# VectorE's score banks moved into three-bank iterations, with 30 sets of exponentials

## The chip, the cores and the metric

The kernel runs on one NeuronCore of one Trainium2 chip. The metric is the device time of one launch in microseconds (us). A profiled execution is one such launch with the hardware profiler on; its span runs from the first to the last instruction.

## The reference

Two branches act on the same kind of input, and a gate mixes them. Branch A is softmax attention with 32 heads of 20 columns over 2048 positions, branch B is a dense layer, a mish, and a dense layer.

```python
x = A_x                                  # 1 x 2048 x 640, bfloat16
g = sigmoid((x * gate_w).sum(-1, keepdims=True))

# branch A: H = 32 heads, Dh = 20
q, k, v = split_heads(x @ wqkv)          # each 1 x 32 x 2048 x 20
p = softmax(einsum("bhqd,bhkd->bhqk", q, k) * Dh ** -0.5)
a = merge_heads(einsum("bhqk,bhkd->bhqd", p, v)) @ wo

# branch B: F = 1536
h = B_x @ w1 + b1
b = (h * tanh(softplus(h))) @ w2         # softplus as log1p(exp(-|h|)) + max(h, 0)

return g * a + (1 - g) * b
```

The kernel reads one x for both branches.

## The kernel before

**Tiling.** Four heads make one value of `p` (eight in all), and a head's 20 columns sit on 32 partitions, so that four heads fill 128. The 2048 queries are cut into four chunks `qc` of 512, the keys into 16 blocks `j` of 128. A pair `(p, qc)` is a *group* `G`; there are 32 groups, in the order of the list `groups`. In a group, a *unit* is one block of keys of one head: 128 keys by 512 queries, one PSUM bank of scores. A *set* is the four units (four heads `t`) of one `j`. There are 32 x 16 x 4 = 2048 units.

**The inner loop.** Units are dealt to iterations of three and two banks in turn (`WIDTHS = (3, 2)`). `emit_qk` issues an iteration's score matmuls (L1070) into the PSUM tile S0 (three banks) or S1 (two banks); `emit_exp` issues one ScalarE instruction over the whole tile (L1081) and writes the exponentials to `E`; `emit_set` multiplies a set of four units into `acc` (L1128). A score matmul uses 32 rows of the array, the rows of its head, and the matmuls of one iteration go to different heads. The value tile `VA` has a column of ones per head, so `acc` also holds the softmax's denominator; `normalise` transposes it (L1096), inverts (L1102), multiplies (L1105, into `T2`) and transposes back (L1114).

**VectorE's exponentials.** In the 27 groups of `JV_GROUPS` the last set (`j = 15`) does not go to ScalarE. `jv_chain` issues one score matmul (L702) into a bank of the general pool `pp`, and a VectorE instruction (L711) that rounds the scores to 16-bit integers in `E_dve`. After the fourth, `jv_steps` lists seven VectorE instructions on all four units at once (128x2048, L730 to L752) that turn the integers into bfloat16 exponentials with the temporaries `w_dve` and `u_dve`. `emit_jv` then multiplies them with `VB`, which is `VA`'s block scaled by a power of two on GpSimd (`scale_v`, L1230).

**What sets the order.** The schedule is written out by the Python program itself: every engine runs its instructions in the order of issue. The program keeps an estimated time for each engine in `T` and decides by it. All other work is cut into `Chain`s: the projections for q and k (L464, read at L475 and L479) and v (L492, L505), the dense layers of branch B (L581 and L612, read at L592 and L624), the output projection (L657, L674), the bound checks (L798), and the four `jv_chain`s of a group. A chain has a start, a due iteration and a lead by which it is sorted (24 for `jv_chain`), takes one of the two banks of `pp`, and ends in a VectorE read of that bank (`evac`). After each iteration `pump` issues pieces of chains, as far as the estimated end of the next exponential allows; where nothing else can run and the estimated activity of TensorE is below 0.54 it issues filler matmuls on the tile `busy` (L1014). VectorE's longer sequences (mish at L530 to L562, the normalising, `jv_steps`) wait in the list `slow`; `run_slow` issues those steps that fit ahead of a given time, the earliest deadline first.

```python
S_full[i] = T["pe"] + NS_SCORES_SEEN
...
limit = T["act"] + NS_EXP[iters[min(i + 1, NI - 1)][1]] - NS_SCORES_SEEN - 60.0
```

A second path, `attention_with_maximum`, follows for inputs that fail a bound; it does not run here.

Of the kernel before, what the change touches and what calls it, by code (L numbers as in the profile page):

```python
# [9 lines left out]
P = 128  # L10
ACT = mybir.ActivationFunctionType
ALU = mybir.AluOpType
# [138 lines left out]
def kernel(  # L151
# [25 lines left out]
    LN2 = 0.6931471805599453  # L177
    Q_SCALE = 512.0 * float(DH) ** -0.5 / LN2
    WIDTHS = (3, 2)
    JV_GROUPS = list(range(4, 31))  # L180
    JV_BIAS = 32
    LEAD_JV = 24
    N_CAP = 1.0e9
    NCELL = 48
    CELLS_KEPT = 2
# [32 lines left out]
    ident = consts.tile([P, P], BF16, tag="ident")  # L218
    wqp = [consts.tile([P, KT, 4, 32], BF16, tag=f"wqp{i}", name=f"wqp{i}") for i in range(2)]
    wkp = [consts.tile([P, KT, 4, 32], BF16, tag=f"wkp{i}", name=f"wkp{i}") for i in range(2)]  # L220
    T2 = [consts.tile([P, QC], BF16, tag=f"T2_{i}", name=f"T2_{i}") for i in range(2)]
    cells = [consts.tile([P, QC], BF16, tag=f"cell{i}", name=f"cell{i}") for i in range(NCELL)]
    busy = consts.tile([P, P], BF16, tag="busy")
    xn = consts.tile([P, NQC], F32, tag="xn")
    wn = consts.tile([P, NQ, 2], F32, tag="wn")
    vn = consts.tile([P, 3], F32, tag="vn")
    F16, I16 = mybir.dt.float16, mybir.dt.int16
    E_dve = consts.tile([P, 4, QC], BF16, tag="E_dve")
    w_dve = consts.tile([P, 4, QC], F16, tag="w_dve")
    VB = consts.tile([P, H, DH + 1], BF16, tag="VB")  # L230
    u_dve = consts.tile([P, 4, QC], F16, tag="u_dve")
    b_dram = tc.dram_tile([S, D], BF16, name="b_dram")
    acc = accpool.tile([P, QC], F32, tag="acc")

# [26 lines left out]
        if u < 2:  # L261
            load_strip(1 - u, 0, eng)
    make_identity(nc, ident)
    warm = consts.tile([P, 1], F32, tag="warm")
    nc.vector.memset(warm, 0.0)
    nc.vector.memset(busy, 1.0)
    nc.scalar.activation(warm, warm, ACT.Exp)
    for t in (wqp[0], wkp[0], VA[:, :, :, DH : DH + 1], wqp[1], wkp[1], T2[0], T2[1]):
        nc.vector.memset(t, 1.0 if len(t.shape) == 4 and t.shape[-1] == 1 else 0.0)
    nc.gpsimd.dma_start(out=wv0[:, :, :], in_=wrows[:, :, 2 * D : 2 * D + 4 * DH])  # L270
    for c in range(1, NQC):
# [27 lines left out]
    for G, (p, qc) in enumerate(groups):  # L299
        first.setdefault(p, G)  # L300

    JV = NS - 1
    with_jv = [G in JV_GROUPS for G in range(len(groups))]
    units = [
        (G, p, qc, j, t)
        for G, (p, qc) in enumerate(groups)
        for j in range(NS)
        if not (with_jv[G] and j == JV)
        for t in range(4)
    ]  # L310
    unit_at = {(G, j): k for k, (G, _, _, j, t) in enumerate(units) if t == 0}
    iters = []
    pos = 0
    while pos < len(units):
        n = min(WIDTHS[len(iters) % len(WIDTHS)], len(units) - pos)
        iters.append((pos, n))
        pos += n
    NI = len(iters)
    it_of = [0] * len(units)
    for i, (a, n) in enumerate(iters):  # L320
# [72 lines left out]
            full = pp.tile([P, QC], F32, tag="pp", name="ps")  # L393
        return full

    def steps(start, parts, deadline):


        seq[0] += 1
        slow.append([deadline, seq[0], start, deque(parts)])  # L400

    def run_slow(limit):

        while True:
            todo = [x for x in slow if max(T["dve"], x[2]) + x[3][0][0] <= limit]
# [284 lines left out]
    EXP_A, EXP_B = 17.79869142, 3.99584201  # L690
    EXP_C = 0.0057399568925583745
    ROUND = 1.5 * 2.0**23
    jv_free = [True]
    jv_at = {}

    def jv_chain(G, p, t, start, due):
        box = {}
        bank = opener(box, QC)

        def piece():  # L700
            jv_free[0] = False
            nc.tensor.matmul(  # L702
                bank()[:, :],
                lhsT=kT[p][32 * t : 32 * t + 32, JV * P : (JV + 1) * P],
                rhs=qT[G][32 * t : 32 * t + 32, :],
                tile_position=(32 * t, 0),
            )

        def finish():
            evac(690)  # L710
            nc.vector.tensor_scalar(  # L711
                out=E_dve.bitcast(I16)[:, t, :], in0=box["ps"][:, :], scalar1=ROUND,
                scalar2=ROUND - 512.0 * JV_BIAS, op0=ALU.add, op1=ALU.subtract,
            )
            if t == 3:
                left = (it_at(G + 1) - now[0]) * 1115.0
                steps(T["dve"], jv_steps(G), T["act"] + left - 4000.0)

        def ready():
            return G in qT and (jv_free[0] if t == 0 else not jv_free[0])  # L720

        return Chain(start, due, [(215, piece)], finish, ready, hard=False, bank=bank, lead=LEAD_JV)

    def jv_steps(G):
        V = nc.vector
        E, w, u = (t.rearrange("p a n -> p (a n)") for t in (E_dve, w_dve, u_dve))
        e, wi = E.bitcast(I16), w.bitcast(I16)

        def mantissa():
            V.tensor_scalar(  # L730
                out=wi, in0=e, scalar1=511, scalar2=0x4000, op0=ALU.bitwise_and, op1=ALU.bitwise_or
            )

        def exponent():
            V.tensor_scalar(
                out=e, in0=e, scalar1=-512, scalar2=2, op0=ALU.bitwise_and, op1=ALU.logical_shift_right
            )

        def square():
            V.tensor_tensor(out=w, in0=w, in1=w, op=ALU.mult)  # L740

        def factor():
            V.tensor_scalar(out=u, in0=w, scalar1=EXP_A, scalar2=EXP_C, op0=ALU.add, op1=ALU.mult)

        def factor2():
            V.tensor_scalar(out=w, in0=w, scalar1=EXP_B, scalar2=None, op0=ALU.add)

        def product():
            V.tensor_tensor(out=w.bitcast(BF16), in0=w, in1=u, op=ALU.mult)

        def scale():
            V.tensor_tensor(out=e, in0=e, in1=wi, op=ALU.add)  # L752
            jv_at[G] = T["dve"] + NS_SEEN

        return [
            (700, mantissa), (700, exponent), (1230, square), (700, factor), (700, factor2),
            (1230, product), (1230, scale),
        ]


# [131 lines left out]
    for G, (p, qc) in enumerate(groups):  # L892
        if with_jv[G]:
            for t in range(4):
                x = it_at(G) + 1 + 2 * t
                chains.append(jv_chain(G, p, t, x, x + 2))

    def spread(a, b, n):
        return [(a + (b - a) * k / n, a + (b - a) * (k + 1) / n) for k in range(n)]
# [152 lines left out]
    E_of = {}  # L1052
    S_free = {}
    S_full = {}
    E_full = {}
    late = [0.0]

    def emit_qk(i):
        a, n = iters[i]
        w = WIDTHS[i % len(WIDTHS)]  # L1060
        tag = f"S{i % len(WIDTHS)}"
        ps = spool.tile([P, w * QC], F32, tag=tag, name="Sp")
        S_of[i] = ps
        T["pe"] = max(T["pe"], S_free.get(tag, 0.0))
        S_full[i] = T["pe"] + NS_SCORES_SEEN
        worked(T["pe"], 215.0, 0.5)
        T["pe"] += NS_SCORES
        for k in range(n):
            G, p, qc, j, t = units[a + k]
            nc.tensor.matmul(  # L1070
                ps[:, k * QC : (k + 1) * QC],
                lhsT=kT[p][32 * t : 32 * t + 32, j * P : (j + 1) * P],
                rhs=qT[G][32 * t : 32 * t + 32, :],
                tile_position=(32 * t, 0),
            )

    def emit_exp(i):
        a, n = iters[i]
        which = i % len(WIDTHS)
        E = ep[which].tile([P, WIDTHS[which] * QC], BF16, tag=f"E{which}", name="E")  # L1080
        nc.scalar.activation(  # L1081
            E[:, 0 : n * QC], S_of.pop(i)[:, 0 : n * QC], ACT.Exp, scale=LN2 / 512.0
        )
        late[0] += max(0.0, S_full[i] - T["act"])
        T["act"] = max(T["act"], S_full.pop(i)) + NS_EXP[n]
        S_free[f"S{i % len(WIDTHS)}"] = T["act"] + NS_EXP_SEEN
        for k in range(n):
            E_of[a + k] = E[:, k * QC : (k + 1) * QC]
            E_full[a + k] = T["act"] + NS_EXP_SEEN

    def normalise(G, p, qc):
# [6 lines left out]
        t2 = T2[G % 2]  # L1098
        OT[(p, qc)] = cells.pop()

        def invert():
# [16 lines left out]
    pv_next = [0]  # L1118
    pv_group = [(0, 0, 0)]
    pv_sets = [0]  # L1120
    jv_in = [False]

    def emit_set(G, p, qc, j, moving, full, VB=None):
        n = pv_sets[0]
# [12 lines left out]
        if n == NS - 1:  # L1137
            normalise(G, p, qc)
            pv_sets[0] = 0
            jv_in[0] = False  # L1140

    def emit_jv(G, p, qc):
        jv_in[0] = jv_free[0] = True
        emit_set(G, p, qc, JV, lambda t: E_dve[:, t, :], jv_at[G], VB)

    def emit_pv(limit):
        count = 0
        while True:
# [8 lines left out]
            if with_jv[G] and not jv_in[0]:  # L1157
                last = pv_sets[0] == NS - 1
                if last and full and G not in jv_at:
                    run_slow(float("inf"))  # L1160
                if pv_sets[0] > 0 and (jv_at.get(G, 1e9) <= T["pe"] + 60.0 or (last and full)):
                    emit_jv(G, p, qc)
                    count += 1
                    continue
# [62 lines left out]
        )  # L1227

    def scale_v(h0, h1):
        nc.gpsimd.tensor_scalar(  # L1230
            out=VB[:, h0:h1, :], in0=VA[:, JV, h0:h1, :], scalar1=2.0**-JV_BIAS, scalar2=None,
            op0=ALU.mult,
        )

    def clear_wo(p):
        if p == 0:
# [7 lines left out]
            nc.sync.dma_start(out=wo_sb[0][32 * t : 32 * t + DH, :, :], in_=rows[t])  # L1244

    at(it_at(first[1]) + 2, gate_values)
    at(it_at(first[1]), lambda: scale_v(4, 16))
    at(it_at(first[4]), lambda: scale_v(16, H))
    at(it_at(1), lambda: nc.vector.tensor_copy(b1f, b1bf))
# [91 lines left out]
```

## Time and profile before

| what | value |
|---|---|
| three timed runs | 945.32 us median, 940.99 to 949.07 |
| the profiled execution | 954.2 us, span 952.3 us |
| granted TensorE clock, mean over the span | 0.962 |
| ScalarE busy | 912.2 us (96%) |
| TensorE matmuls busy | 863.2 us (91%) |
| VectorE busy | 694.3 us (73%) |
| GpSimd busy | 21.7 us (2%) |
| first and last exponential (L1081) | start at 10.4 us, end at 941.2 us |

Busy time is the union of an engine's instructions. In the rows of the profile, the part after the first bar is busy time and mean duration of one instruction, the part after the second is the time the engine stood idle just before these instructions, with the instruction that ended most of it. Matmuls overlap in the array, and a ScalarE instruction's record can begin before its neighbour's has ended, so a mean duration is not the distance from one to the next. A table by stretches gives start and end of a stretch, its length, the busy time and the count of instructions of each engine in it, then the granted TensorE clock and two DMA columns.

### The profile page before, as it was taken

How to read it: one execution, taken by the hardware profiler on the slowest of the kernel's cores; microseconds unless marked ns; L12 is line 12 of the kernel's file. 1: busy time of each engine (PE TensorE's matmuls, PEld its weight loads, DVE VectorE, ACT ScalarE, POOL GpSimd, SP SyncE). 2: the span in 40 equal slices, each digit the busy share in tenths (PEclk: the TensorE clock that was granted, in tenths of full speed). 3: DMA queues.
4: the chain of work that ended last, by engine and by line, in shares of the span. 5: the costliest groups of instructions: out<-in, count | busy, mean ns of one | idle time of the engine just before them, and what ended most of it. 6: DMA issues, size and time to landing. Idle time of an engine off the chain costs nothing.

```text
span 952.3 us, 14757 instructions
## 1 busy us (share of the span) xinstructions
PE 863.2 (91%) x6073; PEld 298.8 (31%) x6073; DVE 694.3 (73%) x1156; ACT 912.2 (96%) x830; POOL 21.7 (2%) x35
## 2 busy tenths in 40 slices
PE   8999989999998888899899989898999899999996
PEld 4443322222233232322223222232223223333332
DVE  4335487777888888777788988788787877876533
ACT  6999998989999999989999999999999989999995
POOL 5000010000000000000000000000000000000000
PEclk9999997979999999979999999999999989999998
DMA  9000010000100010001011001010000000000100
GB/s 289 8 1 1 21 30 1 18 4 1 31 4 19 2 30 1 21 1 50 1 30 35 22 1 30 1 50 1 21 1 21 1 1 15 35 15 9 42 28 30
DMA packets 25632, 21.96 MB, mean 23 GB/s; under 512 B 10089, under 2 KB 24313, under 8 KB 25561
## 3 DMA queue, kind: packets, MB, share of 16 engines
q1 hardware_dynamic: 22808, 14.28, 5.5%
q0 software_dynamic: 1520, 5.94, 2.0%
q8 instruction: 48, 0.79, 0.3%
q10 hardware_dynamic: 1232, 0.76, 0.3%
q14 instruction: 24, 0.19, 0.1%
HBM read 15.73 MB, written 5.24 MB: 22 GB/s over the span
## 4 chain that ended last, share of the span: by engine, by line
ACT 61%; issue 18%; PE 18%; DVE 1%; DMA 1%; POOL 1%; ACTq 0%; POOLq 0%
ACT E L1081 58%; PE Sp L1070 5%; PE acc L1128 3%; ACT e L522 3%; PE ps L657 2%; PE ps L612 2%; PE ps L581 2%; PE ps L464 2%; DMA wv<-in_A_wqkv_dram 1%; PE ps L702 1%; PE ps L1014 0%; PE ps L492 0%; DVE ot L1291 0%; DVE h L592 0%; POOL xs L272 0%
## 5 line engine op out<-in xcount | busy, mean ns | idle before, releaser
L1081 ACT ACTIVATE E<-Sp 128x1536 bf16<-128x1536 f32 (+1 forms) x776 | 894.5, 1351 | 21.9 <-PE Sp L1070 20.8
L1070 PE MATMUL Sp<-qT,kT 32*128 32x512 bf16 x1940 | 313.2, 392 | 76.6 <-ACT E L1081 65.5
L1070 PEld LDWEIGHTS <-kT 32*128 32x128 bf16 x1940 | 104.0, 91 | 306.4 <-issue 287.9
L1128 PE MATMUL acc<-E,VA 128*21 128x512 bf16 x1940 | 196.6, 395 | 0.8 <-DVE T L1096 0.8
L1128 PEld LDWEIGHTS <-VA 128*21 128x21 bf16 x1940 | 47.8, 89 | 113.0 <-issue 112.7
L711 DVE TENSOR_SCALAR E_dve<-ps 128x512 int16<-128x512 f32 x108 | 71.8, 678 | 12.7 <-PE ps L702 12.3
L581 PE MATMUL ps<-xT,w1t 128*128 128x512 bf16 x240 | 80.3, 406 | 0.0
L1014 PE MATMUL ps<-busy 128*128 128x512 bf16 x246 | 75.5, 389 | 0.0
L612 PE MATMUL ps<-w_sb,cell 128*128 128x320 bf16 x384 | 75.3, 307 | 0.0
L592 DVE TENSOR_SCALAR h<-ps,b1f 128x512 f32<-128x512 f32 x48 | 35.8, 746 | 37.5 <-PE ps L581 37.2
L464 PE MATMUL ps<-xT,wkp 128*128 128x512 bf16 x155 | 49.1, 405 | 1.7 <-DVE xT L430 0.8
L464 PE MATMUL ps<-xT,wqp 128*128 128x512 bf16 x155 | 48.4, 392 | 0.0
L657 PE MATMUL ps<-wo_sb,cell 128*128 128x320 bf16 x248 | 46.9, 305 | 0.0
L544 DVE RECIPROCAL r<-r 128x128 f32<-128x128 f32 x48 | 45.4, 945 | 1.0
L479 DVE CAST kT<-ps 128x512 bf16<-128x512 f32 x31 | 21.4, 690 | 32.2 <-PE ps L464 32.1
L475 DVE TENSOR_SCALAR qT<-ps 128x512 bf16<-128x512 f32 x31 | 21.4, 692 | 27.1 <-PE ps L464 26.9
L612 PEld LDWEIGHTS <-cell 128*128 128x128 bf16 x384 | 30.0, 98 | 34.3 <-issue 27.6
L1096 DVE STREAM_TRANSPOSE T<-acc 128x512 f32<-128x512 f32 x32 | 22.9, 715 | 23.0 <-PE acc L1128 22.8
L702 PE MATMUL ps<-qT,kT 32*128 32x512 bf16 x108 | 38.3, 387 | 0.0
L522 ACT ACTIVATE e<-h 128x512 f32<-128x512 f32 x48 | 35.5, 739 | 0.7 <-DVE h L592 0.7
L505 DVE CAST VA<-ps 128x80 bf16<-128x80 f32 (+2 forms) x48 | 16.4, 378 | 25.0 <-PE ps L492 24.9
L553 DVE TENSOR_TENSOR e<-e,r 128x512 f32<-128x512 f32 x48 | 33.2, 692 | 1.6
(107 smaller groups left out, 694.3 us busy)
## 6 DMA issues: line engine op xcount, KB each, us to landing
w1t<-in_B_w_dram SPq DMA_DIRECT2D x14, 480.0 KB, 3.7
b_dram<-Bt SPq DMA_DIRECT2D x4, 640.0 KB, 3.1
out_dram<-ot SPq DMA_DIRECT2D x14, 160.0 KB, 1.8
xs<-in_A_x_dram POOLq DMA_DIRECT2D x3, 640.0 KB, 6.7
w_sb<-in_B_w_dram POOLq DMA_DIRECT2D x1, 1920.0 KB, 12.6
ws<-in_A_wqkv_dram SPq DMA_DIRECT2D x13, 100.0 KB, 3.9
w1t<-in_B_w_dram POOLq DMA_DIRECT2D x2, 480.0 KB, 8.8
wo_sb<-in_A_wo_dram SPq DMA_DIRECT2D x4, 200.0 KB
```

The costliest lines, as they stand in the source:

```text
L464: nc.tensor.matmul(box["ps"][:, :], lhsT=wpad[:, kt, :, :].rearrange("p h d -> p (h d)"), rhs=xT[:, kt, chunk * QC : (chunk + 1) * QC], st ...
L522: nc.scalar.activation(e[:, :], h[:, :], ACT.Exp)
L544: V.reciprocal(out=r[:, Q], in_=r[:, Q])
L581: nc.tensor.matmul(box["ps"][:, :], lhsT=w1t[4 * c + ft // 3][:, kt, (ft % 3) * P : (ft % 3 + 1) * P], rhs=xT[:, kt, c * QC : (c + 1) * QC ...
L612: nc.tensor.matmul(box["ps"][:, :], lhsT=act[(ft, c)][:, u * P : (u + 1) * P], rhs=w2_sb[:, ft, half * HALF : (half + 1) * HALF], start=(f ...
L657: nc.tensor.matmul(box["ps"][:, :], lhsT=OT[(p, c)][:, u * P : (u + 1) * P], rhs=wo_sb[0][:, p, cols], start=(k == 0), stop=(k == len(ps_l ...
L702: nc.tensor.matmul(bank()[:, :], lhsT=kT[p][32 * t : 32 * t + 32, JV * P : (JV + 1) * P], rhs=qT[G][32 * t : 32 * t + 32, :], tile_positio ...
L711: nc.vector.tensor_scalar(out=E_dve.bitcast(I16)[:, t, :], in0=box["ps"][:, :], scalar1=ROUND, scalar2=ROUND - 512.0 * JV_BIAS, op0=ALU.ad ...
L1014: nc.tensor.matmul(ps[:, 0:n], lhsT=busy[:, :], rhs=busy_row(n), start=True, stop=True)
L1070: nc.tensor.matmul(ps[:, k * QC : (k + 1) * QC], lhsT=kT[p][32 * t : 32 * t + 32, j * P : (j + 1) * P], rhs=qT[G][32 * t : 32 * t + 32, :] ...
L1081: nc.scalar.activation(E[:, 0 : n * QC], S_of.pop(i)[:, 0 : n * QC], ACT.Exp, scale=LN2 / 512.0)
L1128: nc.tensor.matmul(acc[32 * t : 32 * t + DH + 1, :], lhsT=VA[:, j, 4 * p + t, :] if VB is None else VB[:, 4 * p + t, :], rhs=moving(t), st ...
```

## The change

- The score matmul of VectorE's set no longer goes through a chain and a bank of `pp`. In 120 of the three-bank iterations ScalarE takes two banks, and the third bank is a score of VectorE's set. `JV_GAPS` says how many iterations pass before each of a group's four; `t` is chosen among the heads left, at first from those that the iteration does not already use.
- `jv_read` issues VectorE's read of that bank right behind the score matmuls of the iteration. The PSUM tile is free for the next scores when ScalarE and VectorE have both read it.
- VectorE's set is in 30 groups (1 to 30), one set each, where there were 27 (4 to 30).
- `E_dve` has two buffers; `w_dve` and `u_dve` hold two units instead of four; the seven steps run once for each half of a set (128x1024), the first half after the second read. The halves are kept in order by the name `"exp"` in `run_slow`.
- `VB` holds two blocks, and `scale_v` fills both; it is called once more, for the first four heads. `T2` is one tile instead of two, and `warm` is a column of `xn`.

```diff
-    JV_GROUPS = list(range(4, 31))
+    JV_SETS = {G: 1 for G in range(1, 31)}
     JV_BIAS = 32
-    LEAD_JV = 24
+    JV_GAPS = {1: (4, 2, 4, 2), 2: (3, 2, 2, 2, 2, 2, 2, 2)}
...
-    E_dve = consts.tile([P, 4, QC], BF16, tag="E_dve")
-    w_dve = consts.tile([P, 4, QC], F16, tag="w_dve")
-    VB = consts.tile([P, H, DH + 1], BF16, tag="VB")
-    u_dve = consts.tile([P, 4, QC], F16, tag="u_dve")
+    E_dve = [consts.tile([P, 4, QC], BF16, tag=f"E_dve{i}", name=f"E_dve{i}") for i in range(2)]
+    w_dve = consts.tile([P, 2, QC], F16, tag="w_dve")
+    VB = consts.tile([P, 2, H, DH + 1], BF16, tag="VB")
+    u_dve = consts.tile([P, 2, QC], F16, tag="u_dve")
...
     while pos < len(units):
-        n = min(WIDTHS[len(iters) % len(WIDTHS)], len(units) - pos)
+        i = len(iters)
+        G = units[pos][0]
+        n = min(WIDTHS[i % len(WIDTHS)], len(units) - pos)
+        x = None
+        got = taken_by.setdefault(G, [])
+        sets_here = len(mine_of[G])
+        if n == 3 and len(got) < 4 * sets_here:
+            since = i - (got[-1][0] if got else iters_start.get(G, i))
+            if since >= JV_GAPS[sets_here][len(got)] and units[pos + 1][0] == G:
+                mine = {units[pos][4], units[pos + 1][4]}
+                k, slot = divmod(len(got), 4)
+                left = [t for t in range(4) if t not in [y for _, y in got[4 * k :]]]
+                t = min(left, key=lambda t: (t in mine, t))
+                got.append((i, t))
+                x = (G, units[pos][1], k, t, slot)
+                n = 2
...
+        extra.append(x)
         pos += n
...
-    def jv_chain(G, p, t, start, due):
...
+    def jv_read(G, k, t, slot, ps, full):
+        if slot == 0:
+            n = jv_set[(G, k)] = len(jv_set)
+            assert n < 2 or n - 2 in jv_emitted, (G, k)
+        n = jv_set[(G, k)]
+        jv_slot[(G, k, t)] = slot
+        run_slow(full + 100.0)
+        vec(690, full)
+        nc.vector.tensor_scalar(
+            out=E_dve[n % 2].bitcast(I16)[:, slot, :], in0=ps, scalar1=ROUND,
+            scalar2=ROUND - 512.0 * JV_BIAS, op0=ALU.add, op1=ALU.subtract,
+        )
+        if slot % 2 == 1:
+            left = (it_at(G + 1) - now[0]) * 1115.0
+            due = T["act"] + (min(left - 4000.0, 9000.0) if k < len(mine_of[G]) - 1 else left - 4000.0)
+            steps(T["dve"], jv_steps(G, k, slot // 2), due, "exp")
...
-            (700, mantissa), (700, exponent), (1230, square), (700, factor), (700, factor2),
-            (1230, product), (1230, scale),
+            (380, mantissa), (380, exponent), (640, square), (380, factor), (380, factor2),
+            (640, product), (640, scale),
...
     def emit_qk(i):
...
+        todo = [(units[a + k][0], units[a + k][1], units[a + k][3], units[a + k][4]) for k in range(n)]
+        if extra[i] is not None:
+            G, p, k, t, slot = extra[i]
+            todo.append((G, p, mine_of[G][k], t))
+        for k, (G, p, j, t) in enumerate(todo):
...
+        if extra[i] is not None:
+            G, p, k, t, slot = extra[i]
+            jv_read(G, k, t, slot, ps[:, n * QC : (n + 1) * QC], S_full[i])
+            S_read[i] = T["dve"] + 60.0
...
+        if i in S_read:
+            S_free[tag] = max(S_free[tag], S_read.pop(i))
...
     def scale_v(h0, h1):
-        nc.gpsimd.tensor_scalar(
-            out=VB[:, h0:h1, :], in0=VA[:, JV, h0:h1, :], scalar1=2.0**-JV_BIAS, scalar2=None,
-            op0=ALU.mult,
-        )
+        for k in range(2):
+            nc.gpsimd.tensor_scalar(
+                out=VB[:, k, h0:h1, :], in0=VA[:, NS - 1 - k, h0:h1, :], scalar1=2.0**-JV_BIAS,
+                scalar2=None, op0=ALU.mult,
+            )
...
+    at(it_at(1), lambda: scale_v(0, 4))
```

More of the change, by code (lines that the diff above doesn't have):

```diff
@@ L220 @@
     wkp = [consts.tile([P, KT, 4, 32], BF16, tag=f"wkp{i}", name=f"wkp{i}") for i in range(2)]
-    T2 = [consts.tile([P, QC], BF16, tag=f"T2_{i}", name=f"T2_{i}") for i in range(2)]
+    T2 = consts.tile([P, QC], BF16, tag="T2")
     cells = [consts.tile([P, QC], BF16, tag=f"cell{i}", name=f"cell{i}") for i in range(NCELL)]
@@ L263 @@
     make_identity(nc, ident)
-    warm = consts.tile([P, 1], F32, tag="warm")
+    warm = xn[:, 0:1]
     nc.vector.memset(warm, 0.0)
@@ L267 @@
     nc.scalar.activation(warm, warm, ACT.Exp)
-    for t in (wqp[0], wkp[0], VA[:, :, :, DH : DH + 1], wqp[1], wkp[1], T2[0], T2[1]):
+    for t in (wqp[0], wkp[0], VA[:, :, :, DH : DH + 1], wqp[1], wkp[1], T2):
         nc.vector.memset(t, 1.0 if len(t.shape) == 4 and t.shape[-1] == 1 else 0.0)
@@ L300 @@
         first.setdefault(p, G)
-    JV = NS - 1
-    with_jv = [G in JV_GROUPS for G in range(len(groups))]
+    mine_of = [[NS - 1 - k for k in range(JV_SETS.get(G, 0))] for G in range(len(groups))]
     units = [
@@ L307 @@
         for j in range(NS)
-        if not (with_jv[G] and j == JV)
+        if j not in mine_of[G]
         for t in range(4)
@@ L312 @@
     iters = []
+    extra = []
     pos = 0
+    taken_by, iters_start = {}, {}
     while pos < len(units):
-        n = min(WIDTHS[len(iters) % len(WIDTHS)], len(units) - pos)
+        i = len(iters)
[14 more added lines that the diff above has]
+                n = 2
+        for k in range(pos, pos + n):
+            iters_start.setdefault(units[k][0], i)
         iters.append((pos, n))
+        extra.append(x)
         pos += n
+    assert all(len(taken_by[G]) == 4 * len(mine_of[G]) for G in range(len(groups)))
     NI = len(iters)
@@ L394, in take_bank, with steps @@
         return full
-    def steps(start, parts, deadline):
+    def steps(start, parts, deadline, line=None):
         seq[0] += 1
-        slow.append([deadline, seq[0], start, deque(parts)])
+        slow.append([deadline, seq[0], start, deque(parts), line])
     def run_slow(limit):
         while True:
-            todo = [x for x in slow if max(T["dve"], x[2]) + x[3][0][0] <= limit]
+            heads = {}
+            for x in slow:
+                heads.setdefault(x[4] or x[1], x)
+            todo = [x for x in heads.values() if max(T["dve"], x[2]) + x[3][0][0] <= limit]
             if not todo:
@@ L692, with jv_steps @@
     ROUND = 1.5 * 2.0**23
-    jv_free = [True]
+    jv_set = {}
     jv_at = {}
-    def jv_chain(G, p, t, start, due):
[L697 to L706, printed above, removed]
-            )
[L709 to L724, printed above, removed]
+    jv_slot = {}
+    halves = {}
+    jv_emitted = set()
+    def jv_read(G, k, t, slot, ps, full):
[14 more added lines that the diff above has]
+            steps(T["dve"], jv_steps(G, k, slot // 2), due, "exp")
+    def jv_steps(G, k, half):
         V = nc.vector
-        E, w, u = (t.rearrange("p a n -> p (a n)") for t in (E_dve, w_dve, u_dve))
+        E, w, u = (
+            t.rearrange("p a n -> p (a n)")
+            for t in (E_dve[jv_set[(G, k)] % 2][:, 2 * half : 2 * half + 2, :], w_dve, u_dve)
+        )
         e, wi = E.bitcast(I16), w.bitcast(I16)
@@ L752, in scale @@
             V.tensor_tensor(out=e, in0=e, in1=wi, op=ALU.add)
-            jv_at[G] = T["dve"] + NS_SEEN
+            halves[(G, k)] = halves.get((G, k), 0) + 1
+            if halves[(G, k)] == 2:
+                jv_at[(G, k)] = T["dve"] + NS_SEEN
         return [
-            (700, mantissa), (700, exponent), (1230, square), (700, factor), (700, factor2),
-            (1230, product), (1230, scale),
+            (380, mantissa), (380, exponent), (640, square), (380, factor), (380, factor2),
+            (640, product), (640, scale),
         ]
@@ L890 @@
         )
[L892 to L896, printed above, removed]
     def spread(a, b, n):
@@ L1054 @@
     S_full = {}
+    S_read = {}
     E_full = {}
@@ L1067, in emit_qk @@
         T["pe"] += NS_SCORES
-        for k in range(n):
-            G, p, qc, j, t = units[a + k]
+        todo = [(units[a + k][0], units[a + k][1], units[a + k][3], units[a + k][4]) for k in range(n)]
[3 more added lines that the diff above has]
+        for k, (G, p, j, t) in enumerate(todo):
             nc.tensor.matmul(
@@ L1085, in emit_exp @@
         T["act"] = max(T["act"], S_full.pop(i)) + NS_EXP[n]
-        S_free[f"S{i % len(WIDTHS)}"] = T["act"] + NS_EXP_SEEN
+        tag = f"S{i % len(WIDTHS)}"
+        S_free[tag] = T["act"] + NS_EXP_SEEN
+        if i in S_read:
+            S_free[tag] = max(S_free[tag], S_read.pop(i))
         for k in range(n):
@@ L1097, in normalise @@
         rec = tp.tile([P, NS], F32, tag="rec", name="rec")
-        t2 = T2[G % 2]
+        t2 = T2
         OT[(p, qc)] = cells.pop()
@@ L1120 @@
     pv_sets = [0]
-    jv_in = [False]
+    jv_in = [0]
     def emit_set(G, p, qc, j, moving, full, VB=None):
@@ L1139, in emit_set @@
             pv_sets[0] = 0
-            jv_in[0] = False
+            jv_in[0] = 0
     def emit_jv(G, p, qc):
-        jv_in[0] = jv_free[0] = True
-        emit_set(G, p, qc, JV, lambda t: E_dve[:, t, :], jv_at[G], VB)
+        k = jv_in[0]
+        n = jv_set[(G, k)]
+        jv_in[0] += 1
+        jv_emitted.add(n)
+        E = E_dve[n % 2]
+        emit_set(
+            G, p, qc, mine_of[G][k], lambda t: E[:, jv_slot[(G, k, t)], :], jv_at[(G, k)], VB[:, k, :, :]
+        )
     def emit_pv(limit):
@@ L1156, in emit_pv @@
             G, p, qc = pv_group[0]
-            if with_jv[G] and not jv_in[0]:
-                last = pv_sets[0] == NS - 1
-                if last and full and G not in jv_at:
+            k = jv_in[0]
+            if k < len(mine_of[G]):
+                last = pv_sets[0] == NS - len(mine_of[G]) + k
+                if last and full and (G, k) not in jv_at:
                     run_slow(float("inf"))
-                if pv_sets[0] > 0 and (jv_at.get(G, 1e9) <= T["pe"] + 60.0 or (last and full)):
+                if pv_sets[0] > 0 and (jv_at.get((G, k), 1e9) <= T["pe"] + 60.0 or (last and full)):
                     emit_jv(G, p, qc)
@@ L1229, in scale_v @@
     def scale_v(h0, h1):
-        nc.gpsimd.tensor_scalar(
-            out=VB[:, h0:h1, :], in0=VA[:, JV, h0:h1, :], scalar1=2.0**-JV_BIAS, scalar2=None,
-            op0=ALU.mult,
-        )
+        for k in range(2):
+            nc.gpsimd.tensor_scalar(
+                out=VB[:, k, h0:h1, :], in0=VA[:, NS - 1 - k, h0:h1, :], scalar1=2.0**-JV_BIAS,
+                scalar2=None, op0=ALU.mult,
+            )
     def clear_wo(p):
```

## The prediction

> **What bounds the kernel now.** I read the page first (busy shares and the chain that ended last), then ScalarE's rows with shapes kept apart, then the stretches where the granted clock was one half, and last TensorE's rows in the window just ahead of such a stretch. The page:
>
> ```profile
> span 952.3 us, 14757 instructions
> PE 863.2 (91%) x6073; PEld 298.8 (31%) x6073; DVE 694.3 (73%) x1156; ACT 912.2 (96%) x830; POOL 21.7 (2%) x35
> PEclk9999997979999999979999999999999989999998
> ACT E L1081 58%; PE Sp L1070 5%; PE acc L1128 3%; ACT e L522 3%; PE ps L657 2%; PE ps L612 2%; PE ps L581 2%; PE ps L464 2%; DMA wv<-in_A_wqkv_dram 1%; PE ps L702 1%; PE ps L1014 0%; PE ps L492 0%; DVE ot L1291 0%; DVE h L592 0%; POOL xs L272 0%
> L711 DVE TENSOR_SCALAR E_dve<-ps 128x512 int16<-128x512 f32 x108 | 71.8, 678 | 12.7 <-PE ps L702 12.3
> L702 PE MATMUL ps<-qT,kT 32*128 32x512 bf16 x108 | 38.3, 387 | 0.0
> ```
>
> The line of exponentials on ScalarE (L1081) is the chain. Its two shapes:
>
> ```profile
> L1081 ACT ACTIVATE E<-Sp 128x1536 bf16<-128x1536 f32 x388 | 607.8, 1567 | 6.4 <-PE Sp L1070 5.8
> L1081 ACT ACTIVATE E<-Sp 128x1024 bf16<-128x1024 f32 x388 | 440.6, 1136 | 15.5 <-PE Sp L1070 15.0
> ```
>
> The rows' means overlap their neighbours, so I took end to end from the trace: the medians are 1343 ns for three banks, 916 for two and 510 for the exponential at L522. So one bank is 427 ns and an instruction 62. The work is 388 x (1.343 + 0.916) + 48 x 0.51 = 901.0 us. From the first start at 10.4 us to the last end at 941.2 us there are 930.7 us, so **29.7 us** of ScalarE's time are lost. Of them 22.1 us lie in and just behind nine stretches, 64.9 us long together, in which TensorE had half its clock; 2.6 us lie before 40 us; the rest is scattered. Three of the nine stretches, and TensorE's rows in the 3.41 us ahead of one:
>
> ```profile
> core 0: us, PE busy (x) PEld busy (x) DVE busy (x) ACT busy (x) POOL busy (x), PEclk, DMA share, GB/s
> 138.47:155.54 17.07, 16.03 (x73) 3.82 (x72) 11.34 (x19) 12.95 (x11) 0.00 (x0) 0.50 0.08 16
> ...
> 404.71:418.37 13.66, 13.66 (x60) 3.18 (x59) 8.39 (x14) 10.17 (x10) 0.00 (x0) 0.50 0.01 1
> ...
> 466.15:469.57 3.42, 3.42 (x16) 0.73 (x14) 1.59 (x4) 2.31 (x2) 0.00 (x0) 0.50 0.00 0
> ```
> ```profile
> L1070 PE MATMUL Sp<-qT,kT 32*128 32x512 bf16 x8 | 1.2, 380 | 0.9 <-ACT E L1081 0.7
> L581 PE MATMUL ps<-xT,w1t 128*128 128x512 bf16 x2 | 0.8, 486 | 0.0
> L1128 PE MATMUL acc<-E,VA 128*21 128x512 bf16 x8 | 0.8, 386 | 0.0
> L702 PE MATMUL ps<-qT,kT 32*128 32x512 bf16 x2 | 0.8, 379 | 0.0
> L464 PE MATMUL ps<-xT,wqp 128*128 128x512 bf16 x1 | 0.4, 379 | 0.0
> ```
>
> In a stretch ScalarE is busy 71 to 76% and TensorE nearly always. Ahead of it TensorE is not idle either, but the work is thin: the two L702 matmuls stand alone on 32 rows, and almost nothing uses the whole array (L464 once; L581 reaches in at the end). I cut the span from 30 to 935 us at full clock into the same 3.41 us windows, on whose grid all stretches begin and end. 173 windows hold no L702 matmul, and none of them was followed by half clock. 25 hold at least about two, and nine of these were, all nine cases. The share of a window that matmuls on the full array stream is 5 to 12% ahead of the nine, 33% in the median of the 173. So the thin phase is made by the four score matmuls of VectorE's set: each takes a bank of the two general ones, waits for VectorE to free it, and keeps other work out meanwhile.
>
> **The change, part by part.**
>
> *ScalarE's work.* Three more groups go to VectorE: 12 banks less, 1928 instead of 1940. But 120 three-bank iterations now give ScalarE only two. Following the list-building code by hand, there are 819 iterations: 290 of three banks, 529 of two. 290 x 1.343 + 529 x 0.916 = 874.0 against 876.5: **-2.5 us** (12 x 0.427 saved, 43 more instructions at 0.062 paid).
>
> *The lone score matmuls.* The 108 at L702 and their claims on the two general banks go; the scores ride in an iteration whose three matmuls take 0.39 us together, as one alone does. In 30 of the 120 the third shares its 32 rows with one of the other two and may run after it, at most 30 x 0.39 = 11.7 us of TensorE; it lies behind the 0.47 us by which three-bank scores are ready before ScalarE (median in the trace). The freed pieces go to full-array work. A pair with an extra bank is 1.83 us long; two score sets and one set at L1128 take 1.2 us by the 0.39 rows, but only 0.33 each start to start as the timeline has them, so 0.6 to 0.8 us remain, two to three pieces of 0.22 us (four at L464 in the trace start within 0.65 us). That is a quarter to a third of full-array work where the nine windows had 5 to 12%. So I let the half-clock stretches go: bounds 0 and **-22.1 us**; I take the whole, and leave room for about one stretch of the new kernel's own, 22.1 / 9 = 2.5 us, taken as **+2 us**.
>
> [...] The windows above show the clock halved after TensorE had been busy 2.4 to 2.9 of 3.41 us, so here I go by the trace.
>
> *The score bank waits for VectorE.* This is the new wait. The bank triple is free when ScalarE and the read (0.68, L711) are both done; behind a late read stand the next three scores and with them all of TensorE, and on VectorE itself the copies out of the general banks. Budget: scores are full 0.05 + 0.39 us after the previous exponential on the triple ends; the two-bank exponential in between ends 0.47 later, the triple's own 0.92 later. 1.39 - 0.68 = 0.71 us of lateness hold nothing, and 0.47 more only eat the slack: ScalarE idles from 1.19 us on. How late are such reads now? From the end of the L702 matmul to the start of L711 it is 0.19 us in the median, 0.63 at 90%, 1.06 at most at full clock. So the lower price is nothing; the upper, a tenth of 120 reads late by 0.3 us beyond the budget, is 3.6. I take **+2 us**.
>
> *VectorE's steps.* These rows price the halves:
>
> ```profile
> L740 DVE TENSOR_TENSOR w_dve<-w_dve 128x2048 f16<-128x2048 f16 x27 | 32.8, 1216 | 0.0
> ...
> L531 DVE TENSOR_SCALAR r<-e 128x512 f32<-128x512 f32 x48 | 20.7, 431 | 1.7
> ...
> L735 DVE TENSOR_SCALAR E_dve<-E_dve 128x2048 int16<-128x2048 int16 x27 | 18.6, 689 | 0.5
> ```
>
> A set now takes 4 x 0.69 + 3 x 1.22 = 6.41 us. Instructions on 128x1024 of two bytes are not in the trace; exact halves would be 3.2 us a half set, no saving 6.41. The nearest rows have the same bytes: L531 0.431, and L553 with two sources 0.692. So a half is 4 x 0.431 + 3 x 0.692 = 3.80, a set 7.60. 30 x 7.60 - 27 x 6.41 = +55 us (bounds +19 and +212), and 12 more reads +8: VectorE goes from 694 to 757 us, 81% of the span. It is off the path: groups 4 to 30 use some 21 to 25 us of 28 to 30, and get 1.2 more; the three early groups use 12.5 to 19 and get 10.3. The cover is its idle time, 258 us, most of it waits for TensorE. The two-fold E_dve takes away the wait for the previous set; the single T2 and w_dve, u_dve are used on VectorE alone, in its order: 0.
>
> *GpSimd.* scale_v issues six instructions instead of two, about 1 us each (L1230, 0.95), at a 2% busy engine, over 5 us ahead of their reader: 0. No DMA is added or moved. One memset less ahead of the first exponential, 0.27 us that lie beside the input's DMAs: 0.
>
> **Sum.** The profiled execution took 954.2 us with a span of 952.3. 954.2 - 2.5 - 22.1 + 2 + 2 = 933.6. The three runs have a median of 945.32 and a lowest of 940.99: the profiled execution is 9 above, and its own lost time is what varies. With less half clock in the plain runs there is less to win, but the end is the same floor, 929.6 with no stretch and 933.6 with my two additions. I go between, toward the floor since plain runs lie below the profiled one: **931 us**, own range 922 to 936.
>
> **The rivals.** (a) *Half clock stays.* The stretches follow a group's start by 5 to 10 us, where other things happen too (the normalising, L1096), and 16 of the 25 windows did not trip; if these set it, only -2.5 + 2 remains: 945 us. For it: two-bank pairs give fewer pieces per iteration. Against: no window without L702 tripped. Chance 0.18. (b) *VectorE becomes the bound*, slower. Place: groups 4 to 30, reads at fixed iterations behind mish steps. Now those groups have 22 to 25 us of work and the waits for TensorE beside it (some 208 us by the groups' idle rows, 6.5 each): 29 of 28 to 30. If the waits do not shrink when 1.2 us come in, each of 27 groups grows by about 1.1, 30 us on 931: 961 us. It decides where reads start later than 1.19 us after the scores. Against: most reads start within 0.33. Chance 0.12. (c) The change not doing what it says would be scores still alone; the list has 120 extras, so I leave it no share.
>
> **How the numbers follow.** Forecast 0.70, (a) 0.18, (b) 0.12. The range reaches down to the floor with all 29.7 us back, 954.2 - 29.7 - 2.5 = 922, one less for scatter, and up past (a) to 948: 921 to 948, leaving out (b) and little else. About 1% is what a measurement of this kernel can tell from no change: 935.9 to 954.8. Faster gets 0.66 of the forecast and 0.02 of (a); same 0.04, 0.16 and 0.02 of (b); slower 0.10.
>
> **What would show it.** Right: clock near 1.0 through the middle; two ACTIVATE rows, 290 and 529; idle before L1081 under 8 us; VectorE near 757; reads of the third bank starting within 0.7 us. Wrong: half-clock stretches some 5 to 10 us into groups (a), or scores waiting on the read, with TensorE idle "<-DVE E_dve" over 20 us (b).

## The result and the profile after

The changed kernel takes **981.56 us** (median of 4 runs, 980.70 to 982.79); the kernel before, beside it, 944.60. The ratio is 1.039, 95% interval 1.034 to 1.044: slower by 4%, where I had forecast 931 us. The ratios, here and below, leave out executions more than 1.5% above the fastest of the same kernel; the medians are over all.

The page of the changed kernel, with the lines that answer to those shown of before (L1107 is the exponential, L734 VectorE's read, L1092 the scores):

```profile
span 979.4 us, 15290 instructions
PE 874.1 (89%) x6184; PEld 311.6 (32%) x6184; DVE 744.3 (76%) x1398; ACT 916.8 (94%) x873; POOL 24.4 (2%) x39
PEclk9999999999999999999999999999999999999998
ACT E L1107 52%; PE Sp L1092 8%; DVE E_dve L734 7%; ACT e L548 3%; PE acc L1157 2%; PE ps L490 2%; PE ps L638 1%; PE ps L607 1%; DMA wv<-in_A_wqkv_dram 1%; DVE h L618 1%; PE ps L518 0%; PE ps L683 0%; DVE ot L1329 0%; DVE T L1125 0%; DVE kT L505 0%
```

Two things stand out. The clock row is full until the last slice (mean 0.995), as forecast. And VectorE's read L734 has 7% of the chain, where L711, VectorE's read of before, is not among the lines shown. ScalarE's rows and the head of the chip's waits (engine, line, whom it waited for, us in total, times, longest) tell where it sits:

```profile
L1107 ACT ACTIVATE E<-Sp 128x1024 bf16<-128x1024 f32 x529 | 548.5, 1061 | 43.3 <-DVE E_dve L734 40.8 <-PE Sp L1092 1.3 <-PE acc L1157 1.0
L1107 ACT ACTIVATE E<-Sp 128x1536 bf16<-128x1536 f32 x290 | 438.2, 1511 | 0.8 <-PE Sp L1092 0.8
```
```profile
DVE E_dve L734 <- PE Sp L1092: 62.2, 93, 1.5
ACT E L1107 <- DVE E_dve L734: 40.8, 107, 1.5
```

ScalarE's exponential waits for VectorE's read *of the other bank of the same tile*, 107 times. VectorE itself is not late: it sits idle ahead of 93 of its 120 reads until the scores are there. One extra iteration in the timeline:

```profile
261.60 0.39 PE L1092 MATMUL Sp<-qT,kT 32*128 32x512 bf16 x3
...
262.04 0.69 DVE L734 TENSOR_SCALAR E_dve<-Sp 128x512 int16<-128x512 f32 x1 [0.65 <-PE Sp L1092]
...
262.77 1.94 ACT L1107 ACTIVATE E<-Sp 128x1024 bf16<-128x1024 f32 x2 [0.36 <-DVE E_dve L734]
```

Scores are there at 261.99, the read starts 0.05 us later, ends at 262.73, and only then the exponential starts. In the trace the exponential's record starts 33 ns after the read's end in the median, and the read starts 43 ns after the scores (0.11 us at 95%). Against the steady 0.916 us an extra iteration costs ScalarE 0.405 us more in the median, 0.59 in the median of the 30 whose third matmul shares its rows (that matmul starts 0.215 us late), **52.9 us** in all 120. The sum then closes: 954.2 (profiled before) - 2.5 (ScalarE's work) - 21.4 (stalls in half-clock stretches, 22.3 to 0.9) + 52.9 = 983.2, beside 981.2 for the profiled execution.

The programs' instruction lists show the same without a time. The built program names for each instruction the semaphores that it waits for, each by the engine whose instructions raise it (`PE_49` TensorE's, `DVE_49` VectorE's, `Activation_49` ScalarE's). In ScalarE's list of the changed kernel all 120 extra iterations wait on VectorE's semaphore alone (all 120 reads of VectorE wait on TensorE's), the other 699 on TensorE's, 407 of them on ScalarE's own too; the middle line is one of the 120:

```
44 L1107 Activation E<-Sp 128x1024 [waits PE_49,Activation_49]
45 L1107 Activation E<-Sp 128x1024 [waits DVE_49]
46 L1107 Activation E<-Sp 128x1024 [waits PE_49,Activation_49]
```

### The profile page after: what moved, and what is told of

It is laid out like the page before. It is cut to its first block, busy times and chain, and to the rows that moved or that the text cites. A ratio compares the mean times of both kernels' runs of the same rounds, so it can differ in the third digit from the quotient of the medians.

```text
span 979.4 us, 15290 instructions
## 1 busy us (share of the span) xinstructions
PE 874.1 (89%) x6184; PEld 311.6 (32%) x6184; DVE 744.3 (76%) x1398; ACT 916.8 (94%) x873; POOL 24.4 (2%) x39
## 4 chain that ended last, share of the span: by engine, by line
ACT 55%; issue 17%; PE 16%; DVE 11%; DMA 1%; POOL 1%; POOLq 0%; ACTq 0%; DVEq 0%
ACT E L1107 52%; PE Sp L1092 8%; DVE E_dve L734 7%; ACT e L548 3%; PE acc L1157 2%; PE ps L490 2%; PE ps L638 1%; PE ps L607 1%; DMA wv<-in_A_wqkv_dram 1%; DVE h L618 1%; PE ps L518 0%; PE ps L683 0%; DVE ot L1329 0%; DVE T L1125 0%; DVE kT L505 0%
## 5 line engine op out<-in xcount | busy, mean ns | idle before, releaser
L1107 ACT ACTIVATE E<-Sp 128x1024 bf16<-128x1024 f32 (+1 forms) x819 | 896.4, 1220 | 44.1 <-DVE E_dve L734 40.8
L1092 PE MATMUL Sp<-qT,kT 32*128 32x512 bf16 x2048 | 326.4, 382 | 90.4 <-ACT E L1107 75.6
L1092 PEld LDWEIGHTS <-kT 32*128 32x128 bf16 x2048 | 115.5, 91 | 330.7 <-issue 307.9
L734 DVE TENSOR_SCALAR E_dve<-Sp 128x512 int16<-128x512 f32 x120 | 82.9, 691 | 63.2 <-PE Sp L1092 62.2
L1032 PE MATMUL ps<-busy 128*128 128x512 bf16 x357 | 110.3, 384 | 0.0
L771 DVE TENSOR_TENSOR w_dve<-w_dve,u_dve 128x1024 bf16<-128x1024 f16 x60 | 41.1, 686 | 0.9
L774 DVE TENSOR_TENSOR E_dve<-E_dve,w_dve 128x1024 int16<-128x1024 int16 x60 | 41.1, 685 | 0.9
L1032 PEld LDWEIGHTS <-busy 128*128 128x128 bf16 x357 | 26.9, 97 | 44.6 <-issue 35.1
L762 DVE TENSOR_TENSOR w_dve<-w_dve 128x1024 f16<-128x1024 f16 x60 | 41.0, 684 | 0.0
L588 DVE TENSOR_TENSOR cell<-h,e 128x512 bf16<-128x512 f32 x48 | 33.0, 687 | 1.1
```

Of the source, the lines that this page charges most:

```text
L734: nc.vector.tensor_scalar(out=E_dve[n % 2].bitcast(I16)[:, slot, :], in0=ps, scalar1=ROUND, scalar2=ROUND - 512.0 * JV_BIAS, op0=ALU.add, ...
L1032: nc.tensor.matmul(ps[:, 0:n], lhsT=busy[:, :], rhs=busy_row(n), start=True, stop=True)
L1092: nc.tensor.matmul(ps[:, k * QC : (k + 1) * QC], lhsT=kT[p][32 * t : 32 * t + 32, j * P : (j + 1) * P], rhs=qT[G][32 * t : 32 * t + 32, :] ...
L1107: nc.scalar.activation(E[:, 0 : n * QC], S_of.pop(i)[:, 0 : n * QC], ACT.Exp, scale=LN2 / 512.0)
```

## The experiments

Theory S: in the built program two engines' reads of one PSUM tile run one after the other, in the order of issue, though they touch different banks; ScalarE comes second and pays. It is then a wait that the program contains, not two reads that hinder each other. Rivals: L, VectorE has too much work, so reads are late and hold the score bank (my rival (b)); R, the third score matmul is late. Theory T is about the half clock: it comes from windows that lone score matmuls leave without full-array work.

**e1: the read behind the exponential.**

```diff
 emit_qk:   # of an extra iteration
-            jv_read(G, k, t, slot, ps[:, n * QC : (n + 1) * QC], S_full[i])
 emit_exp:  # behind nc.scalar.activation
+            jv_read(G, k, t, slot, ps[:, n * QC : (n + 1) * QC], T["act"])
```

> After, with VectorE's read of the third bank issued behind the two-bank exponential of the same iteration instead of ahead of it; nothing else moves. Theory S (in the changed kernel the two reads of one PSUM tile run one after the other in the order of issue, and ScalarE pays since it comes second): ScalarE no longer waits for VectorE, and VectorE's read begins when the exponential ends. Then the tile is free 0.72 us later than the exponential (0.03 to start, 0.69 for the read), the next scores on it are full at 0.05 + 0.72 + 0.39 = 1.16 us, ScalarE's two-bank exponential in between ends at 0.92, so some 0.3 us remain of the 0.44 lost per extra iteration: 120 x 0.3 = 36 in place of 53, about 965 us (958 to 972), and the profile puts ScalarE's idle time down to TensorE's scores. Theory L (VectorE is too busy: its reads come late and hold the bank): the order of two issues changes nothing, 977 to 985 us. Theory R (the third score matmul is late since 30 of 120 share rows): also 977 to 985.

Measured: 993.24 us, ratio 1.054 (1.048 to 1.060). The waits turn round, which only S has, but the time goes up:

```profile
DVE E_dve L734 <- ACT E L1104: 64.8, 95, 2.7
PE Sp L1092 <- DVE E_dve L734: 58.5, 117, 1.1
ACT E L1104 <- PE Sp L1092: 51.4, 133, 1.3
```

Now the reader that comes second is VectorE, TensorE waits for it with the next scores on the tile, and ScalarE waits for those: 0.405 us in the median two iterations on, 49.8 us in all, where I had 0.3 and 36. The time lies outside what either side had expected (958 to 972, 977 to 985). I had left out that an exponential after a wait takes 1.02 us to its end and not 0.916. Another 15.6 us lie in five half-clock stretches; that TensorE's new waits brought these back is likely, but no run shows it apart. So the order of issue decides who waits, but not that someone does.

**e2: a tile of its own for the third bank.**

```diff
-        ps = spool.tile([P, w * QC], F32, tag=tag, name="Sp")
+        ps = spool.tile([P, 2 * QC], F32, tag=tag, name="Sp")
+        third = spool.tile([P, QC], F32, tag="SJ", name="Sj") if n + (extra[i] is not None) == 3 else None
...
+        if n == 3:
+            nc.scalar.activation(E[:, m : m + QC], third[:, :], ACT.Exp, scale=LN2 / 512.0)
```

> After, with the three-bank tile cut into a tile of two banks and a tile of one; a plain three-bank iteration takes two exponentials (two banks, one bank), an extra iteration one exponential on the first tile and VectorE's read on the second. Same iterations, same VectorE work. Theory S: no tile has two readers, so the 53 us of the extra iterations go, and 290 more ScalarE instructions cost 0.062 each, 18 us: 981.6 - 53 + 18 = about 947 us (942 to 954); extra iterations show a two-bank period of 0.92 us. Theory L: VectorE has the same work at the same places, so the reads still hold ScalarE up: 981 + 18 = about 999. Theory R: the same, about 999.

Measured: 953.66 us, ratio 1.013 (1.007 to 1.019). VectorE's work and its reads' places are those of after, and 28 us are gone in spite of 290 more ScalarE instructions:

```profile
L1110 ACT ACTIVATE E<-Sp 128x1024 bf16<-128x1024 f32 x819 | 832.7, 1152 | 5.6 <-PE Sj L1093 1.8 <-PE acc L1160 1.6 <-PE Sp L1093 1.1
L1112 ACT ACTIVATE E<-Sj 128x512 bf16<-128x512 f32 x290 | 210.3, 725 | 0.0
```

No wait for VectorE is left in ScalarE's rows. L and R, which asked for 999, fall. The time is near the upper end of 942 to 954: against exponentials that run back to back ScalarE loses 11.7 us here, in the changed kernel 5.5 outside the extra iterations.

**e3: two and two banks, and one for VectorE alone.**

```diff
-    WIDTHS = (3, 2)
+    WIDTHS = (2, 2)
...
+            third = spool.tile([P, QC], F32, tag="SJ", name="Sj")
+            T["pe"] = max(T["pe"], S_free.get("SJ", 0.0))
```

> After, with iterations of two and two banks in two tiles, and a fifth bank as a tile of its own for VectorE's scores alone, again 120 of them in groups 1 to 30, never on rows that the iteration uses. Theory S: 964 two-bank exponentials at 0.916 are 883 us where 819 mixed ones were 874; with 24.5 us of mish exponentials, 11.3 us ahead of the first, 11 behind the last and 2 around the span this is 932, and some 5 us of stalls: about 937 us (932 to 945), faster than the kernel before by about 1%, with full clock. Theory L: VectorE's load is that of after, so reads come late again and evacuations with them: over 965 us.

Measured: 954.14 us, ratio 1.010 (1.002 to 1.018), and inconclusive: its executions go from 947.9 us at a mean clock of 0.995 to 1025.8 at 0.889, so the clock covers what was to be seen. Even the best, at full clock, is 11 over the expected 937 and 3 over S's range, though far below L's 965; what the 11 are stays open. Stretches before, in and after the half clock of the longest one (columns as in the table of the prediction):

```profile
300.00:362.30 62.30, 57.37 (x380) 19.55 (x383) 55.50 (x101) 62.30 (x71) 0.98 (x2) 1.00 0.05 12
362.30:584.20 221.90, 216.38 (x877) 44.76 (x888) 124.60 (x229) 156.91 (x159) 3.13 (x4) 0.50 0.06 15
```

**e4: before, with the lone score matmuls four iterations apart.**

```diff
-                x = it_at(G) + 1 + 2 * t
+                x = it_at(G) + 1 + 4 * t
```

> The kernel before, with the four lone score matmuls of a set allowed to start four iterations apart (some 4.5 us) instead of two; all else as it was. Theory T (the half-clock stretches come from windows of 3.41 us that hold two or more lone score matmuls): few such windows are left, half clock falls from 65 us to under 20, and 22 us of lost ScalarE time shrink to some 7: 925 to 937 us in place of 944.6. Rival (the stretches belong to the start of a group, whatever runs there): the clock stays near 0.96 and the time within 940 to 950.

Measured: 964.11 us, ratio 1.023 (1.017 to 1.029). It didn't settle T, since something else broke. Windows with about two lone matmuls fell from 25 to 6, and those that tripped, that is were followed by half clock, from nine to one; but at the end of three groups ScalarE stood idle for 4.6 to 9.2 us, and the clock fell in each of these gaps. The longest one:

```profile
512.46 0.61 PE L1128 MATMUL acc<-E_dve,VB 128*21 128x512 bf16 x4 [3.68 <-DVE E_dve L752]
...
518.56 0.61 PE L1128 MATMUL acc<-E,VA 128*21 128x512 bf16 x4 [5.49 <-DVE T L1096]
...
519.81 2.48 ACT L1081 ACTIVATE E<-Sp 128x1024 bf16<-128x1024 f32 x2 [9.21 <-PE Sp L1070]
```

First TensorE waits for the late set, then for the transpose of `acc` (L1096), which stands behind a whole mish sequence in VectorE's order. TensorE waits for the transpose 4.5 to 5.7 us in all three gaps; in the other two the set is late by 0.3 us at most.

**e5: the changed kernel, its banks handed out anew per iteration.**

```diff
-        ps = spool.tile([P, w * QC], F32, tag=tag, name="Sp")
+        if i % 2 == 0:
+            pool = open_three(f"s0_{i}")     # closes the last pool on these three banks
+            if extra[i] is not None:
+                ps = pool.tile([P, 2 * QC], F32, tag="S0", name="Sp")
+                third = pool.tile([P, QC], F32, tag="SJ", name="Sj")
+            else:
+                ps = pool.tile([P, w * QC], F32, tag="S0", name="Sp")
+        else:
+            ps = spool.tile([P, w * QC], F32, tag=tag, name="Sp")
```

> After, with the same three banks, iterations, instructions and order of issue, but the banks are handed out anew for each three-bank iteration: a plain one gets one tile of three banks, an extra one a tile of two for ScalarE and a tile of one for VectorE. ScalarE then waits for TensorE alone in extra iterations, and the next scores wait for each reader bank by bank. Theory S (the whole loss of after is ScalarE waiting for VectorE's read of another bank of its tile): the 53 us of the extra iterations go and no instruction is added; 981.6 - 53 = 929, and up to 10 more for the scattered stalls that the kernel with a tile of its own showed: 928 to 940, centre 934, half clock at the end only, faster than the kernel before. Theory L (VectorE's load or late reads have a share of the loss): 945 or more.

Measured: **936.83 us**, ratio 0.991 (0.988 to 0.995), inside S's range. ScalarE's list now has `Activation E<-Sp 128x1024 [waits PE_49]` in all 120 extra iterations, and its rows are:

```profile
L1125 ACT ACTIVATE E<-Sp 128x1024 bf16<-128x1024 f32 x529 | 548.8, 1120 | 8.6 <-PE Sp L1110 3.6 <-PE acc L1175 2.1 <-PE Sj L1110 2.0
L1125 ACT ACTIVATE E<-Sp 128x1536 bf16<-128x1536 f32 x290 | 445.7, 1537 | 1.6 <-PE Sp L1110 1.5
```

The counts 529 and 290 are those of the changed kernel, and so are VectorE's instructions (busy 742.0 us for 744.3). In 109 of the 120 the read and the exponential overlap by more than 0.15 us, and neither is slower for it: the read takes 0.692 us, the exponential ends 0.917 after its neighbour. What is lost in extra iterations falls from 52.9 to 2.8 us; the losses elsewhere grow by 8.3, and 4.9 of all that is lost now lie in one half-clock stretch of 10.2 us. The banks are also given back to TensorE one reader at a time here, but TensorE had no wait for L734 in the changed kernel, so that has nothing to win. So the tile that two engines share is the whole of the 4%.

**e6: before, with full-array work beside each lone matmul.**

```diff
         def piece():
             jv_free[0] = False
+            for _ in range(2):
+                nc.tensor.matmul(
+                    bank()[:, :], lhsT=busy[:, :], rhs=busy_row(QC), start=True, stop=True
+                )
...
-        return Chain(start, due, [(215, piece)], finish, ...)
+        return Chain(start, due, [(645, piece)], finish, ...)
```

> The kernel before, with two filler matmuls on the full array (tile busy, 512 columns) issued into the same bank ahead of each of the 108 lone score matmuls, which overwrite it; the planner's price for the piece is raised from 215 to 645 ns. Theory T (half clock comes from windows that the lone matmuls leave without full-array work): every lone matmul brings 0.43 us of full-array work, a window with two of them has at least 25% of it where the nine had 5 to 12%, the stretches go, and with them most of 22 us of lost ScalarE time: mean clock over 0.985 and 926 to 938 us. Rival (the stretches belong to a group's start): clock 0.96 to 0.98, and the 46 us of added TensorE work can only cost: 942 to 955.

Measured: **935.98 us**, ratio 0.990 (0.987 to 0.993), and 0.9 us from the fastest of 11 runs to the slowest, where the kernel before beside it spread over 17 (937.1 to 954.6, 22 runs).

```profile
PEclk9999999999999999999999999999999999999998
```

The half clock of the middle is gone, by adding work that computes nothing. T holds, and it is worth 1% by itself. The rival is out: a group still starts with the same other work, and the clock stays full (mean 0.996). (With the higher price the planner issued 177 fillers of its own instead of 246.) What about the filler counts, that it uses the whole array or only that TensorE is busier, the run doesn't tell apart.

**e7: e5 with six sets more.**

```diff
-    JV_SETS = {G: 1 for G in range(1, 31)}
+    JV_SETS = {G: 2 if G in (1, 2, 3, 28, 29, 30) else 1 for G in range(1, 31)}
```

> The kernel with the banks handed out anew (three-bank tile, or two and one), and two VectorE sets instead of one in the groups 1 to 3 and 28 to 30, where VectorE has room: there it is busy 18 to 25 of 28 us in groups 1 to 3 and 11 to 25 in the last ones. Theory S (ScalarE's work is the bound once it does not wait for VectorE): each set more takes 4 x 0.427 = 1.7 us from ScalarE; the iterations stay 819 or so: 936.8 - 6 x 1.7 = 926.6 us (923 to 931). Theory L (VectorE is close to being the bound, 79% busy in the middle): 62 us more on VectorE come back as late sets and stalls, 934 us or more.

Measured: 1032.73 us, ratio 1.076 (1.067 to 1.085). S fell. L's "934 or more" holds, with late sets as it said, but it gave no size. VectorE is busy 78% of the span, yet in its two-set groups the second set ends after the group, and TensorE and ScalarE wait, as in e4 but longer:

```profile
922.35 0.61 PE L1175 MATMUL acc<-E_dve,VB 128*21 128x512 bf16 x4 [12.22 <-DVE E_dve L783]
...
925.02 2.04 ACT L1125 ACTIVATE E<-Sp 128x1024 bf16<-128x1024 f32 x2 [13.73 <-PE Sp L1110]
```

Four such gaps of 9 to 16 us, and 116 us of ScalarE's time lost in and behind the half clock that follows them. The mean share of busy time gave no sign of it. As e4 and e7 have it, the thing to price is the room between a set's last read and its group's end.

## Why the prediction was wrong

- *ScalarE's work*, -2.5 us: right. The steady work falls from 901.5 to 899.0 us, with 290 and 529 instructions as counted.
- *The lone score matmuls*, -22.1 us, with 2 left over: right. Stalls in half-clock stretches fell from 22.3 to 0.9 us, and one stretch of 3.4 us is left in the middle. e6 shows the cause alone. In e5, without ScalarE's new wait, one stretch cost 4.9 us, more than the 2 that I had left. (In the nine stretches ScalarE was busy 65 to 76%, not 71 to 76 as I had read.) The length of TensorE's idle gaps doesn't tell the two kernels apart: between 40 and 915 us none is longer than 1.4 us before or 1.3 us after, while the granted clock fell to 0.50 nine times there before and once after.
- *The score bank waits for VectorE*, +2 us: this step failed. It measured **52.9**. I asked only who waits for the bank when both reads are done, and gave the read 0.71 us of room from ScalarE's end. I took for granted that the two reads of the tile run side by side, and never priced the wait of the one reader for the other. The reads were as prompt as I had said, even more so (0.043 us in the median against 0.19): a read that starts at once still ends 0.26 us after the previous exponential (0.04 + 0.69 after scores that are 0.47 ahead of it), the exponential starts 0.03 later, and after a wait it needs 0.11 more: 0.40 us, in most of the 120. Each of these numbers but the order was in the profile of before. The order stands in the diff: `jv_read` is issued in `emit_qk`, ahead of `emit_exp`, on a slice of the same `ps`. With the two reads in turn, the late third matmul of the 30 doesn't stay behind the 0.47 us either, as the term above had it: there the stall is 0.59 us.
- *VectorE's steps*, 757 us: 744.3. The half instructions take 0.42 and 0.685 us where I had 0.431 and 0.692. All durations added up grow by 60.8 us, near the 63 that I had; the busy time grows by only 50, since more of VectorE's records overlap their neighbours (44.5 us for 33.8). The steps themselves are off the path, as said.
- *The rivals.* (a) fell, the clock is full. The outcome of (b), slower, came true, its mechanism not: VectorE waited for the scores and not the scores for it. A third mechanism, with the same new wait but the other engine behind it, was missing from my list. The signs I had named for (b), reads later than 1.19 us and TensorE waiting for L734, are both absent.

## What to carry to other kernels

When a second engine begins to read a tile that another reads, ask how the built program orders the two reads, bank or no bank: here different banks of one tile were read in turn, and a tile per reader in the same space gave back 45 us. Look into the waits of the instruction list for the instruction that sets the pace, and price them like any other wait. And look at what TensorE does in the windows ahead of each fall of its clock: two matmuls of filler beside each of the 108 lone ones (935.98 us) were worth as much as the whole rebuilt schedule of e5 (936.83).

## What the runs showed of the hardware

- In the kernel before, TensorE's granted clock fell to 0.50 nine times in the middle, in stretches of 3.41 to 17.07 us that begin and end on a grid of 3.41 us. The window of 3.41 us ahead of each was at full clock, and in it TensorE was busy 2.4 to 2.9 us and matmuls on the full array filled 5 to 12%. No window without lone 32-row matmuls tripped there, and filler beside these removed all nine (e6). A share of the full array that decides does not come out of the traces: before, a window with 6% did not trip (746.05 to 749.46 us, busy 2.51); in the changed kernel one with 12.5% did and others between 11 and 13% did not; in e1, which has no lone score matmul, two with 19% did.
- Half clock lasted although TensorE was busy: in one of e3's four executions the granted clock was 0.50 for 221.9 us, with TensorE busy 216.4 of them, while ScalarE fell to 71%. Why this stretch lasted and those of the kernel before ended after 3.41 to 17.07 us stays open.
- In the kernel before, an exponential of two banks ends 0.916 us after its neighbour when the two run back to back, and takes 1.024 us after a wait; with three banks it is 1.343 and 1.451. So a stall of ScalarE cost 0.11 us here on top of its length.
- In 109 of e5's 120 extra iterations ScalarE and VectorE read different banks of PSUM at the same time, and neither was slower: 0.917 us from end to end for the exponential and 0.692 us for the read, where it was 0.916 back to back and 0.692 in the changed kernel, with the two in turn.
